# The first loads of an attention and channel-mix kernel on other queues: projection and one k on ScalarE's, the other three on SyncE's

## The chip, the cores and the metric

The kernel runs on one core of a Trainium2 chip. A core has five engines that run side by side, each with its own instruction stream: TensorE (PE in the profile, with PEld for its weight loads), VectorE (DVE), ScalarE (ACT), GpSimd (POOL) and SyncE (SP), which here only issues transfers. Transfers (DMA) are issued by an engine into its own queue and carried out by 16 DMA engines. The metric is the time in microseconds (us) that the device takes for the whole kernel; lower is better.

## The reference

Two parts in a row. First an attention whose mask comes from hashing: each row of q and k (4 batches, 8 heads, 768 rows, 64 wide) is multiplied by a projection of 64 x 6, the signs of the six results make a bucket, and a query sees only the keys of its own bucket.

```python
q_bits = (np.einsum('bhsd,dk->bhsk', q, proj) > 0).astype(np.int64)
k_bits = (np.einsum('bhsd,dk->bhsk', k, proj) > 0).astype(np.int64)
...
mask = q_bucket[:, :, :, None] == k_bucket[:, :, None, :]
scores = scale * np.matmul(q, k.transpose(0, 1, 3, 2))
scores = np.where(mask, scores, -1000000000.0)
...
return np.matmul(attn, v).astype(np.float32)
```

Then a channel mix over the heads put side by side (512 wide): each row is blended with the row before it in two ways, one blend goes through a 512 x 1024 product, a squared ReLU and a 1024 x 512 product, the other through a 512 x 512 product and a sigmoid, and the two results are multiplied.

## The kernel before, in words

The 32 heads are worked in 16 pairs. For each pair, q and k are brought into a transposed form (64 rows per head, 768 columns), and six rows of signs are put beside them, so that one product gives score and mask bonus together. A pair has 12 slots, one for each head and each block of 128 keys: a score product (`score`, L491), an exponential on ScalarE (`pt`, L498), and two slots later the product with the values (`pv`, L528). The channel mix of the batch before is worked in between from a list of items. The order of all work on every engine is written out by hand (`tc.manual_schedule`).

The change lies in the start, ahead of the first slot. These are its steps in program order; pair 0 is handled differently from all others, since nothing can hide its loads.

- The projection `projp` is loaded by a DMA that GpSimd issues (L69), ahead of GpSimd's own work: building two identity matrices, four memsets (L221), and a copy of the projection into the other half of the partitions (L230), which waits for that load.
- `load_qk(0)` (L256) loads q and k of pair 0 in four transfers, a head at a time: q of either head on SyncE's queue, k of either head on ScalarE's.
- ScalarE then loads its table of functions and runs one dummy exponential (L971).
- SyncE goes on with v of the first head (L296), q and k of pair 1 (L262), the two mixing vectors (L975), v of the second head, v of pair 1, and q and k of pair 2.
- TensorE multiplies constants (`keep_warm`, L987), nine products of 128 x 384 whose result is not used.
- `turn_pe` (L331) transposes: q of the first head, then k of the first head, three products each, and ScalarE copies each result to `t` (L335). `cast_pe` turns halves of `t` into the score operands `aq` and `ak` on VectorE, GpSimd or ScalarE (L349, L347).
- `turn_pe` for k of the second head; then `bits_first` (L363), eight products of `t` with the projection for the first head's hash bits; then the signs of these: two on ScalarE for q (L374), two on VectorE for k (L403).
- `turn_pe` for q of the second head, and `turn_and_cast` for q of the first head of pair 1.
- Then slot 0 begins with the first score product (L491).

Each engine works strictly in this order; an instruction that waits holds up all behind it on the same engine. SyncE and ScalarE each have one queue of transfers. A transfer signals its end on one of eight semaphores that all transfers of these two queues use in turn, in program order, and a transfer from SyncE that takes a semaphore for the next time waits until its last user has landed.

Of the kernel before, what the change touches and what calls it, by code (L numbers as in the profile page):

```python
# [36 lines left out]
def kernel(  # L37
# [13 lines left out]
    nc = tc.nc  # L51
    B, H, S, D = q.shape
    NB = proj.shape[1]
    DM = H * D
    DF = moe_w_k.shape[1]
    NC_ = S // P
    HALF = S // 2
# [6 lines left out]
    consts = ctx.enter_context(tc.tile_pool(name="consts", bufs=1))  # L64

    projp = consts.tile([P, 64], FP32, name="projp")
    nc.gpsimd.dma_start(out=projp[0:D, 0:NB], in_=proj)  # L69
    ident32 = consts.tile([P, P], FP32, name="ident32")  # L70
    make_identity(nc, ident32)
    ident16 = consts.tile([P, P], BF16, name="ident16")
# [99 lines left out]
    def fast():  # L172
        with ExitStack() as fx:
# [42 lines left out]
            for s in range(NSET):  # L216
                d = {}
# [29 lines left out]
            SRC = (q, k)  # L247

            def load_qk(n):
                b, t = divmod(n, NPB)  # L250
                tl = nat.tile([P, 2, 2, HALF], FP32, name=f"qk{n}", tag="qk")
                nats[n] = tl
                if n == 0:
                    for j in range(2):
                        for i, eng in enumerate((nc.sync, nc.scalar)):
                            eng.dma_start(  # L256
                                out=tl[:, i, j, :],
                                in_=SRC[i][b, 2 * t + j].rearrange("(p c) d -> p (c d)", c=NC_),
                            )
                    return  # L260
                for i in range(2):
                    nc.sync.dma_start(  # L262
                        out=tl[:, i, :, :],
                        in_=SRC[i][b, 2 * t : 2 * t + 2].rearrange(
                            "j (p c) d -> p j (c d)", c=NC_
                        ),
                    )
# [18 lines left out]
            def load_pair(n, sides="qk"):  # L286
                if n < NTE:
                    load_qk(n)
                else:
                    load_blocks(n, sides)  # L290
# [35 lines left out]
            def turn_pe(n, i, j, eng=None):  # L326

                which, tp = take([P, HALF], FP32, f"tp{n}_{i}_{j}")
                for x in range(3):
                    cols = slice(x * P, (x + 1) * P)  # L330
                    nc.tensor.transpose(tp[:, cols], nats[n][:, i, j, cols], ident32)  # L331
                if eng in (None, nc.vector):
                    nc.vector.tensor_copy(t32(n)[:, i, j, :], tp)
                else:
                    eng.copy(t32(n)[:, i, j, :], tp)  # L335
                give(which)
# [629 lines left out]


            load_qk(0)
            warm = rcp.tile([P, 1], FP32, name="warm", tag="warm")
            nc.vector.memset(warm, 0.0)  # L970
            nc.scalar.activation(warm, warm, AF.Exp)  # L971
            load_v(0, (0,))
            load_qk(1)
            for x, src in enumerate((moe_mu_k, moe_mu_r)):
                nc.sync.dma_start(  # L975
                    out=mu_rows[x * NDC : (x + 1) * NDC, :],
                    in_=src.rearrange("(c p) -> c p", p=P),
# [5 lines left out]
            idle = scp.tile([P, 2, 512], FP32, name="idle", tag="sc")  # L983

            def keep_warm(count, to):
                for _ in range(count):
                    nc.tensor.matmul(  # L987
                        to,
                        epsm,
                        epsm[:, None, :].to_broadcast([P, 3, P]),  # L990
                        start=True,
                        stop=True,
                    )
# [2 lines left out]
                take([P, HALF], FP32, f"bf0{side}") for side in "qk"  # L996
            ]
            firsts[0] = bq, bk
            keep_warm(9, idle[:, 0, 0:HALF])
            turn_pe(0, 0, 0, nc.scalar)  # L1000
            turn_pe(0, 1, 0, nc.scalar)
            cast_pe(0, 0, 0, (nc.vector, nc.gpsimd))
# [259 lines left out]
    with tc.manual_schedule():  # L1262
        fast()
# [33 lines left out]
```

## Time and profile before

| | us |
|---|---|
| median of three runs | 248.12 |
| the three runs | 250.88, 247.43, 248.12 |
| the profiled execution | 249.21 |
| span of that execution, first to last instruction | 247.1 |
| TensorE busy in it | 239.0 (97%) |
| ScalarE busy | 207.7 (84%) |
| VectorE busy | 175.6 (71%) |
| GpSimd busy | 115.6 (47%) |

All times inside the kernel are counted from the start of the span. The profile has a page (busy time by engine, the span in 40 slices, DMA queues, the chain of work that ended last, the costliest groups), and the trace behind it answers finer questions: a timeline of instructions in a window, busy time by window, the chain in order of time, who waited for whom. In a line of the timeline stand start, duration, engine, source line, operation, output and inputs, shapes, a count where equal neighbours are merged, and in brackets how long the engine stood idle before it and what ended that. SPq, ACTq and POOL lines with DMA_DIRECT2D are the issuing of a transfer, not the transfer.

### The profile page before, as it was taken

How to read it: one execution, taken by the hardware profiler on the slowest of the kernel's cores; microseconds unless marked ns; L12 is line 12 of the kernel's file. 1: busy time of each engine (PE TensorE's matmuls, PEld its weight loads, DVE VectorE, ACT ScalarE, POOL GpSimd, SP SyncE). 2: the span in 40 equal slices, each digit the busy share in tenths (PEclk: the TensorE clock that was granted, in tenths of full speed). 3: DMA queues.
4: the chain of work that ended last, by engine and by line, in shares of the span. 5: the costliest groups of instructions: out<-in, count | busy, mean ns of one | idle time of the engine just before them, and what ended most of it. 6: DMA issues, size and time to landing. Idle time of an engine off the chain costs nothing.

```text
span 247.1 us, 6715 instructions
## 1 busy us (share of the span) xinstructions
PE 239.0 (97%) x2443; PEld 144.6 (59%) x2443; DVE 175.6 (71%) x416; ACT 207.7 (84%) x343; POOL 115.6 (47%) x216
## 2 busy tenths in 40 slices
PE   5998999999999999999999999999999999999995
PEld 3565766664665556565665656565665656555443
DVE  2776988969896957577594957686697837499522
ACT  4797999999899888889999889889999898629620
POOL 5898885796919082744519182653709100000000
PEclk9999999999999999999999999999999999999999
DMA  6998897496999385776928386775920111120133
GB/s 191 348 219 196 181 209 189 88 208 139 229 158 263 76 239 137 220 170 169 217 61 220 67 220 144 233 157 156 228 73 5 46 46 42 45 86 1 45 109 112
DMA packets 28230, 36.70 MB, mean 149 GB/s; under 512 B 3216, under 2 KB 25376, under 8 KB 28192
## 3 DMA queue, kind: packets, MB, share of 16 engines
q1 hardware_dynamic: 25744, 33.21, 51.8%
q0 software_dynamic: 2160, 2.62, 6.9%
q8 instruction: 20, 0.33, 0.7%
q10 hardware_dynamic: 288, 0.39, 0.5%
q14 instruction: 18, 0.15, 0.2%
HBM read 31.99 MB, written 6.29 MB: 155 GB/s over the span
## 4 chain that ended last, share of the span: by engine, by line
PE 85%; ACT 8%; DMA 4%; issue 1%; SPq 1%; DVE 0%; ACTq 0%
PE sc L491 22%; PE vp L620 17%; PE kp L620 16%; PE oo L528 12%; PE rp L620 8%; ACT pt L498 7%; PE bb L450 4%; DMA qk<-in_q_dram 3%; PE ot L575 2%; DMA aq<-sg 1%; PE tp L331 1%; PE bb L423 1%; PE oo L519 1%; ACT sq L314 0%; SPq L256 0%
## 5 line engine op out<-in xcount | busy, mean ns | idle before, releaser
L498 ACT ACTIVATE pt<-sc 128x768 bf16<-128x768 f32 x192 | 151.0, 815 | 16.1 <-PE sc L491 13.6
L491 PE MATMUL sc<-aq,ak 70*128 70x384 bf16 (+1 forms) x384 | 93.8, 325 | 1.5 <-ACT pt L498 1.1
L528 PEld LDWEIGHTS <-pt 128*128 128x128 bf16 x1152 | 60.6, 97 | 27.0 <-ACT pt L498 0.2
L528 PE MATMUL oo<-va,pt 128*128 128x65 bf16 x1152 | 66.3, 193 | 0.0
L620 PE MATMUL vp<-wv_sb,k 128*128 128x512 bf16 (+2 forms) x200 | 54.7, 370 | 0.0
L620 PE MATMUL kp<-xk,wk_sb 128*128 128x384 bf16 x256 | 53.6, 326 | 0.4 <-DVE ob L548 0.4
L491 PEld LDWEIGHTS <-ak 70*128 70x128 bf16 (+1 forms) x384 | 34.4, 98 | 27.5 <-issue 4.5
L393 POOL TENSOR_SCALAR aq<-t 64x768 bf16<-64x768 f32 x24 | 19.8, 826 | 56.4 <-DVE t L388 47.2
L657 DVE TENSOR_TENSOR k<-kr 128x384 bf16<-128x384 bf16 x64 | 27.0, 433 | 11.3 <-ACT kr L651 10.7
L620 PEld LDWEIGHTS <-wk_sb 128*128 128x128 bf16 x256 | 21.7, 97 | 14.0 <-issue 3.8
L651 ACT ACTIVATE kr<-kp 128x384 bf16<-128x384 f32 x49 | 24.4, 500 | 4.5 <-PE kp L620 4.5
L620 PE MATMUL rp<-wr_sb,xr 128*128 128x512 bf16 x96 | 27.9, 379 | 0.0
L679 DVE SCALAR_TENSOR_TENSOR os<-th,vp 128x512 f32<-128x512 bf16 (+2 forms) x25 | 16.5, 660 | 15.3 <-PE vp L620 11.9
L620 PEld LDWEIGHTS <-k 128*128 128x128 bf16 x200 | 16.8, 98 | 10.6 <-issue 1.2
L393 POOL TENSOR_SCALAR ak<-t 64x768 bf16<-64x768 f32 x24 | 20.5, 853 | 4.5 <-DVE t L388 1.7
L668 ACT ACTIVATE th<-rp 128x512 bf16<-128x512 f32 x24 | 14.3, 595 | 9.8 <-PE rp L620 9.8
L388 DVE STREAM_TRANSPOSE t<-bl 128x768 f32<-128x768 f32 x24 | 22.4, 957 | 0.0
L477 POOL CAST va<-vf 128x384 bf16<-128x384 f32 x32 | 18.3, 573 | 5.3 <-DMA vf<-in_v_dram 4.5
L314 ACT ACTIVATE sq<-bl 128x768 bf16<-128x768 f32 x24 | 20.2, 844 | 0.0
L479 POOL TENSOR_TENSOR s<-vf 128x192 f32<-128x192 f32 x32 | 20.1, 627 | 0.0
L576 DVE COPY xt<-ot 128x768 bf16<-128x768 bf16 x16 | 8.9, 557 | 14.7 <-PE ot L575 14.7
L541 DVE TENSOR_TENSOR su<-oo,vb 128x390 f32<-128x390 f32 x12 | 6.7, 562 | 10.0 <-PE oo L528 10.0
(87 smaller groups left out, 236.8 us busy)
## 6 DMA issues: line engine op xcount, KB each, us to landing
bl<-in_q_dram SPq DMA_DIRECT2D x48, 176.0 KB
bl<-in_k_dram SPq DMA_DIRECT2D x48, 176.0 KB
vf<-in_v_dram SPq DMA_DIRECT2D x15, 384.0 KB
out_dram<-os SPq DMA_DIRECT2D x18, 256.0 KB
out_dram<-os SPq DMA_DIRECT2D x10, 128.0 KB
qk<-in_q_dram SPq DMA_DIRECT2D x3, 384.0 KB
qk<-in_k_dram SPq DMA_DIRECT2D x3, 384.0 KB
wk_sb<-in_moe_w_k_dram POOLq DMA_DIRECT2D x2, 512.0 KB, 6.4
```

Source lines behind the costliest of these rows:

```text
L314: nc.scalar.activation(junk, src, AF.Square, accum_out=acc)
L388: nc.vector.transpose(t32(n)[:, i].rearrange("p h (c f x) -> p (h c) f x", c=3, f=4), src)
L393: eng.tensor_scalar(out=augs[n % NSET]["qk"[i], j][ROWS[j], :], in0=t32(n)[ROWS[j], i].rearrange("p h y -> p (h y)"), scalar1=(1.0, ALPHA)[i],
L477: nc.gpsimd.tensor_copy(to, of)
L479: nc.gpsimd.tensor_add(s3, vf[:, 0 : 3 * D], vf[:, 3 * D : 6 * D])
L491: nc.tensor.matmul(sc[:, sp, 0:HALF], au["k", j][kr, jc * P : (jc + 1) * P], au["q", j][kr, sp * HALF : (sp + 1) * HALF], start=True, stop ...
L498: nc.scalar.activation(pt.rearrange("p (s q) -> p s q", s=2), sc[:, :, 0:HALF], AF.Exp, bias=EXP_BIAS, scale=SCALE / 2.0 if (n, j) == TWIC ...
L528: nc.tensor.matmul(oo[:, ic, :], pts[n, j, jc][:, ic * P : (ic + 1) * P], vas[n % NSET][j][:, jc, :],  start=(late(n) and jc == 0 and ic = ...
L620: nc.tensor.matmul(box["t"], lhs(), rhs(), start=(i == 0), stop=(i == len(mms) - 1))
L651: nc.scalar.activation(kr, kp, AF.Relu)
L657: 1, lambda: nc.vector.tensor_tensor(out=k2, in0=kr, in1=kr, op=ALU.mult)
L679: nc.vector.scalar_tensor_tensor(out=box["os"][:, y], in0=box["th"][:, y], scalar=1.0, in1=vp, op0=ALU.add, op1=ALU.mult,)
```

## The change

Three edits, all at the start. The projection is loaded from ScalarE's queue rather than by GpSimd. Of the four loads of pair 0, ScalarE's queue keeps one, k of the second head, behind the projection; SyncE's takes q of the first head, k of the first head and q of the second, in this order. TensorE multiplies seven constants rather than nine.

```diff
-    nc.gpsimd.dma_start(out=projp[0:D, 0:NB], in_=proj)
+    nc.scalar.dma_start(out=projp[0:D, 0:NB], in_=proj)
...
                 if n == 0:
-                    for j in range(2):
-                        for i, eng in enumerate((nc.sync, nc.scalar)):
-                            eng.dma_start(
-                                out=tl[:, i, j, :],
-                                in_=SRC[i][b, 2 * t + j].rearrange("(p c) d -> p (c d)", c=NC_),
-                            )
+
+                    for i, j, eng in (
+                        (0, 0, nc.sync), (1, 0, nc.sync), (1, 1, nc.scalar), (0, 1, nc.sync)
+                    ):
+                        eng.dma_start(
+                            out=tl[:, i, j, :],
+                            in_=SRC[i][b, 2 * t + j].rearrange("(p c) d -> p (c d)", c=NC_),
+                        )
                     return
...
-            keep_warm(9, idle[:, 0, 0:HALF])
+            keep_warm(7, idle[:, 0, 0:HALF])
```

In `(i, j)`, `i` is 0 for q and 1 for k, and `j` is the head. The order of instructions on TensorE, VectorE and GpSimd is otherwise the same, and so is ScalarE's behind its two transfers.

## The prediction

> **What bounds the kernel now.** I read the page first. Its engine rows make TensorE (PE) the busiest engine by far, and the chain that ended last names it for most of the span; only 4% of that chain is DMA.
>
> ```profile
> PE 239.0 (97%) x2443; PEld 144.6 (59%) x2443; DVE 175.6 (71%) x416; ACT 207.7 (84%) x343; POOL 115.6 (47%) x216
> ...
> PE 85%; ACT 8%; DMA 4%; issue 1%; SPq 1%; DVE 0%; ACTq 0%
> ```
>
> The reader is to see that no steady part of the kernel is touched by this change: all of it lies ahead of the first score product. So the next views are the windows of the start and the same chain there, listed in order of time.
>
> ```profile
> 0.00:8.82 8.82, 5.77 (x32) 3.04 (x33) 2.79 (x22) 4.61 (x9) 5.62 (x20) 1.00 0.76 241
> 8.82:20.00 11.18, 10.79 (x133) 7.20 (x130) 9.48 (x21) 9.93 (x16) 9.81 (x22) 1.00 0.84 233
> ```
>
> ```profile
> 2.14 6.19 DMA qk<-in_q_dram
> 8.33 0.14 issue
> 8.47 0.52 PE tp L331 x3
> 8.98 0.33 PE sc L491 x2
> 9.31 0.78 PE bf L363 x8
> ```
>
> The columns of the windows are length, then busy time and count of PE, PEld, DVE, ACT and POOL, then clock, DMA share and GB/s. From 8.82 us on, PE is busy 10.79 of 11.18 us; before that, 5.77 of 8.82. What the start is worth is therefore decided by when the first score product begins, at 8.82 us. And the chain says what decided that: not a transfer of pair 0, whose order the change rewrites, but the q of **pair 1**, issued at 2.14 and landed at 8.33. PE works in program order, and three transposes of pair 1 stand ahead of the first score.
>
> The timeline shows the other chain that leads to the same score, through pair 0:
>
> ```profile
> 0.74 0.88 SPq L256 DMA_DIRECT2D qk<-in_q_dram  x2
> 0.74 0.90 ACTq L256 DMA_DIRECT2D qk<-in_k_dram  x2
> 1.05 2.99 PE L987 MATMUL idle<-epsm 128*128 128x384 bf16 x9 [1.05 <-DVE epsm L75]
> 1.27 0.74 POOL L69 DMA_DIRECT2D projp<-in_proj_dram  x1 [0.83 <-POOLq L1281]
> ...
> 3.88 0.82 PE L331 MATMUL tp<-ident,qk 128*128 128x128 f32 x6
> 3.96 0.42 POOL L221 MEMSET ak<- 64x384 f32 x1
> ...
> 4.41 0.86 ACT L335 COPY t<-tp 128x384 f32<-128x384 f32 x2 [1.24 <-PE tp L331]
> ...
> 5.30 0.52 ACT L347 ACTIVATE ak<-t 64x384 bf16<-64x384 f32 x1
> ...
> 6.13 0.52 PE L331 MATMUL tp<-ident,qk 128*128 128x128 f32 x3 [1.44 <-DMA qk<-in_k_dram]
> 6.23 0.18 POOL L230 COPY projp<-projp 64x6 f32<-64x6 f32 x1 [1.85 <-DMA projp<-in_proj_dram]
> ...
> 6.58 0.51 PE L363 MATMUL bf0q<-t,projp 64*32 64x384 f32 x1
> ...
> 7.36 0.55 PE L331 MATMUL tp<-ident,qk 128*128 128x128 f32 x3
> ...
> 7.54 0.98 ACT L374 ACTIVATE aq<-bf0q 6x384 bf16<-6x384 f32 x2 [0.36 <-PE bf0k L363]
> ...
> 8.47 0.52 PE L331 MATMUL tp<-ident,qk 128*128 128x128 f32 x3 [0.56 <-DMA qk<-in_q_dram]
> 8.75 0.75 DVE L349 TENSOR_SCALAR aq<-t 64x384 bf16<-64x384 f32 x2
> 8.82 0.49 PE L491 MATMUL sc<-aq,ak 70*128 70x384 bf16 x2
> ```
>
> PE stands still for 1.44 us until k of the second head has landed (6.13), GpSimd 1.85 us until the projection has (6.23); then come the bit products (6.58) and the signs on ScalarE, which end at 7.54 + 0.98 = 8.52. The change shortens this chain, but the other one ends later: had the signs been there early, the score would still have followed the transposes that started at 8.47. The two are only 8.82 - 8.52 = 0.3 us apart, so neither alone can give more than the other lets it.
>
> **The change, part by part.** The *projection* moves from GpSimd's queue to ScalarE's. GpSimd loses 0.74 us of issuing, so its memsets, done at 3.96 + 0.42 = 4.38, end near 3.6; the identity that the transposes need comes early too, at nothing gained, because they wait for q. On ScalarE's queue it takes a slot of 0.90 / 2 = 0.45 us, exactly that of the k which leaves, so k of the second head keeps its place there and the table load behind it does not move. Its landing by this queue is not in the trace. Bounds: the first q and k, some 130 times its bytes, were transposed 3.88 - 0.74 = 3.1 us after their issue; the old way took 4.8 us.
>
> ```profile
> projp<-in_proj_dram POOLq DMA_DIRECT2D x1, 1.5 KB, 4.8
> ```
>
> I take 3.1 (a hardware queue, at the head of it): landed by 3.9, two microseconds before anything can use it. Its copy on GpSimd no longer binds at all.
>
> *k of the first head* goes second on SyncE's queue: issued 0.88 / 2 = 0.44 us later. Before, its transposes were the last three of six, from 3.88 + 0.33 = 4.2 on. Bounds for them now: 0.44 later (4.65), or no later, since half the bytes no longer share the engines ahead of it. I take the late end, as the second head's k now runs beside it on the other queue: the second copy to t ends at 4.41 + 0.86 + 0.44 = 5.7 instead of 5.27. If nothing covered it, it would cost 0.44 us; it is covered by the transfer that ends at 8.33.
>
> *k of the second head* has only the 1.5 KB of the projection ahead of it on its queue instead of a whole head's k. Bounds for its transposes: 6.13 as now, or right behind the first head's, 4.65 + 0.33 = 5.0. I take the early end. The bit products need both copies, so they start near 5.75 instead of 6.58, and the signs, 7.54 - 6.58 = 0.96 behind, would run from 6.7 to 7.7, not 8.52. *q of the second head* is third on SyncE's queue, 0.44 us later; its transposes (7.36) come behind the bit products and can be late by as much without holding the score past 7.7.
>
> *The rest of SyncE's queue*: v, pair 1's q and k and the two mixing vectors are issued 0.44 us later. The q of pair 1 needs 6.19 us from issue to landing with three transfers ahead of it, so it waits in the queue, not for its issue: cost nothing, as long as the engines have other work. A later SyncE transfer waits for the one eight places before it; with one more hardware transfer these pairs shift by one, so v of the second head waits for k of the second head, not for the first q. GpSimd converts that v at 12.30 us:
>
> ```profile
> 12.30 0.51 POOL L477 CAST va<-vf 128x384 bf16<-128x384 f32 x1
> ```
>
> which leaves over 5 us of cover.
>
> So the sum hangs on **when pair 1's q lands**. Ahead of it go the same bytes as before: four transfers of pair 0 and one of v. What the engines moved meanwhile:
>
> ```profile
> 2.00:4.00 2.00, 2.00 (x9) 0.99 (x8) 0.29 (x14) 1.15 (x2) 1.98 (x9) 1.00 0.99 320
> 4.00:6.00 2.00, 0.70 (x7) 0.46 (x5) 0.35 (x1) 1.38 (x3) 0.38 (x2) 1.00 0.86 228
> 6.00:8.00 2.00, 1.78 (x14) 0.77 (x14) 0.42 (x1) 0.94 (x2) 1.54 (x6) 1.00 1.00 357
> ```
>
> Between 4 and 6 us the rate fell to 228 GB/s and the DMA share to 0.86, with work queued. At the 320 of the window before, the 2 us would have carried 184 KB more, which is 184 / 357 = 0.5 us of the rate behind it. In that window the projection's software-built transfer ran beside the others (it landed just before 6.23), so the change removes one suspect; the trace does not show that it was the cause. Bounds for the landing: unchanged, 8.33, or 1.0 us earlier (the dip gone and the engines level). I take 0.5 us earlier, the size of the dip. Then the transposes start near 8.0 and the score near 8.3, still behind the signs of 7.7. Gain 0.5 us; behind 8.82 PE is full, so it goes through to the end.
>
> A rule of the Trainium skill speaks against even that: "DMA: Bandwidth & Descriptors", section "Issuing engines are not separate DMA queues", says that transfers from all engines run on the same 16 DMA engines, so that spreading them saves issue time only. By it the sum would be 0 us. The trace agrees in that 6.19 us of landing stand against 0.44 us of issue.
>
> *Two of nine constant products* go: the nine start 0.32 us apart (from 1.1 to 3.6 us, eight steps), so PE is free at 1.05 + 7 x 0.32 = 3.3 us rather than 3.9. Nothing waits there but the first transposes, gated by q's landing. Alone they are worth 0 to 0.6 us on pair 0's chain, all covered by the transfer of pair 1; I take 0. What they may cost is the second rival.
>
> ```profile
> L987 PE MATMUL idle<-epsm x9: 454/527/528, 1.1 to 3.6; 128*128 128x384 bf16 x9
> ```
>
> Sum: -0.5 us against the profiled execution, 249.21 us (span 247.1 and 2.1 around it), or 248.7. That execution lies 1.1 us above the median of the three runs, 248.12, so the prediction for a median is 248.12 - 0.5 = **247.6 us**.
>
> **The rivals.** *Nothing moves* (the change does not do what it says): pair 1's q lands at 8.33 whatever goes before it, since the bytes are the same, and the dip is chance. For it: the chain's 6.19 us; against it: the dip itself. Time 248.1.
>
> *Slower, by the clock of PE.* The nine products take 0.32 us for 384 columns, while two score products of 384 columns take 0.33 together: PE began at half speed. The transposes at 3.88 ran as fast as those of 10.73, six in 0.82 us, so the clock had risen by then, after 2.8 us of unbroken products. (The window rows give a clock of 1.00 from the first microsecond on, so that column does not show this.)
>
> ```profile
> 10.57 0.33 PE sc L491 x2
> ```
>
> ```profile
> 10.73 0.82 PE L331 MATMUL tp<-ident,qk 128*128 128x128 f32 x6
> ```
>
> Seven products are 7 x 0.32 = 2.2 us. If the clock needs more than that, it stays low through the gaps of the start and rises only in the dense work behind the first score: some 2.8 to 3.4 us of it at half speed loses 1.4 to 1.7 us, and the bit products ahead, 0.8 us longer, up to 0.3 more. It decides from the point where the products stop before the clock has risen and the transfers leave PE idle. Against it: transposes follow at 3.3 to 4.2 and fill up the sum. Time 248.12 + 1.4 to 2.0, say 249.8. For a loss of 2% (5 us) the clock would have to be low for 10 us of dense work.
>
> On the same point the Trainium skill, "TensorE: Matmul & The Clock Gate", Part 1 (the HAM clock gate), states that the clock is released after about 3.4 us of sustained activity, in a free-running window, and its Part 4 that transposes do not count as activity in the same way; by it the release could slip to a later window in some executions. The 2.8 us above agree with a free-running window, and no run here shows yet what seven products do.
>
> *More gain*: the engines run level, pair 1's q lands by 7.3, and the signs at 7.7 decide: 8.82 - 7.7 = 1.1 us, 247.0. Against it: nothing shows that the transfers of pair 0 were what made some engines late.
>
> **How the numbers follow.** My forecast gets 0.45, nothing moves 0.25, the clock 0.20, more gain 0.10. The likeliest alone spans 246.9 to 248.3 (gain between 0 and 1.0, with 0.2 either way for a median). The runs shown reach from 247.43 to 250.88, a scatter wider than the gain; so the range goes from 246.3 (more gain, with the lowest run's 0.7 below the median) to 250.2 (the clock, at its dear end). Over 2% is 5 us, about what a measurement of this kernel can tell from no change. No case reaches it with its own price. Slower gets 0.10: half of the clock's chance, for executions in which it stays low through several gaps. Faster gets 0.04, for what I have not seen; within 2%: 0.86.
>
> **What would show it.** Right: the chain of waits still names the q of pair 1 ahead of the first score, which starts at 8.0 to 8.6 us; GpSimd's copy of the projection starts before 5 us; the transposes of the second head's k start before 5.6; the window 4 to 6 us moves over 270 GB/s. Wrong: a first score at 8.8 with an unchanged landing (nothing moves); transposes or score products of 0.33 us each, not a pair, behind 3.9 us (the clock); a first score before 7.8, with a sign on ScalarE named just ahead of it (more gain).

## The result, and the profile after

| | before | after |
|---|---|---|
| median of 20 runs, us | 248.09 | 249.25 |
| lowest and highest, us | 247.43, 252.85 | 248.04, 250.66 |
| the profiled execution, us | 249.21 | 249.21 |
| its span, us | 247.1 | 247.3 |
| first score product at | 8.82 | 9.57 |
| first score product of pair 1 at | 20.40 | 20.62 |

The change made the kernel slower by 0.4%: the ratio of after to before is 1.0042, with a 95% interval of 1.0024 to 1.0061. The forecast was 0.2% faster. The two profiled executions took the same time, 249.21 us; the one of before lies 1.1 us above its median, the one of after lies at it. So the profiles show where the time is decided, and the medians how much it is.

First the page of after: the engine row, and the chain that ended last by engine.

```profile
PE 239.4 (97%) x2419; PEld 145.6 (59%) x2441; DVE 175.4 (71%) x416; ACT 207.8 (84%) x343; POOL 114.9 (46%) x215
...
PE 90%; ACT 5%; DVE 2%; issue 1%; ACTq 0%
```

The 4% of DMA are gone from the chain. Then the windows of after, up to its first score product and behind it (columns as in the prediction), and the start of its chain in order of time.

```profile
0.00:9.57 9.57, 7.43 (x30) 3.99 (x31) 2.55 (x21) 4.57 (x9) 5.70 (x21) 1.00 0.79 249
9.57:20.00 10.43, 10.39 (x124) 6.81 (x123) 8.93 (x20) 9.16 (x15) 8.12 (x18) 1.00 0.80 223
```

```profile
1.05 2.42 PE idle L988 x7
3.47 1.45 PE tp L332 x6
6.00 0.88 PE tp L332 x3
...
8.31 1.47 PE tp L332 x6
```

TensorE does less work ahead of the first score than before (30 instructions, not 32) and is busy longer, 7.43 us against 5.77. This chain names no transfer, only TensorE's own slow instructions and two of ScalarE's; its link at 6.00 hides a transfer, as the rows below show. The timeline of after shows two faults, a late k and a slow TensorE:

```profile
0.74 0.55 ACTq L68 DMA_DIRECT2D projp<-in_proj_dram  x1
1.33 0.60 ACTq L257 DMA_DIRECT2D qk<-in_k_dram  x1
...
3.40 1.51 PE L332 MATMUL tp<-ident,qk 128*128 128x128 f32 x6
3.59 0.18 POOL L229 COPY projp<-projp 64x6 f32<-64x6 f32 x1 [0.51 <-DMA projp<-in_proj_dram]
...
5.88 0.84 SPq L297 DMA_DIRECT2D vf<-in_v_dram  x2
6.00 0.88 PE L332 MATMUL tp<-ident,qk 128*128 128x128 f32 x3 [1.09 <-ACT ak L348]
6.81 0.85 PE L364 MATMUL bf0q<-t,projp 64*32 64x384 f32 x1
...
8.24 1.54 PE L332 MATMUL tp<-ident,qk 128*128 128x128 f32 x6
9.57 0.79 PE L492 MATMUL sc<-aq,ak 70*128 70x384 bf16 x2
```

The projection is there early, as forecast: GpSimd copies it at 3.59, not 6.23. But k of the second head, whose way was meant to be free, is transposed at 6.00, against 6.13 before and 5.0 in the forecast, and SyncE stands until then as well (5.88; before, it issued v of the second head at 4.17). And everything on TensorE runs at half speed up to the first score: six transposes in 1.51 us instead of 0.82, a product of the bits in 0.85 instead of 0.51. (The bracket of the row at 6.00 names ScalarE. But by the trace's records the k landed at 5.87, SyncE's v at 5.88 waits for the same k, and in a second execution of this kernel, below, the bracket names the transfer.)

The 6.13 of before is itself a late one. By the same records the second head's k landed at 6.00 in that profile, but at 4.78 to 5.47 in the five other profiles below that keep before's queues (with seven, twelve or three products, the gap filled, the later block loads). In the six with after's queues it landed at 5.71 to 6.28. One profile of each kernel therefore hides most of what the change did to this load.

Behind the start nothing differs. This is the first score product of pair 1, in after:

```profile
20.62 0.49 PE L492 MATMUL sc<-aq,ak 70*128 70x384 bf16 x2
```

From it to the end of the span are 247.3 - 20.6 = 226.7 us, and as much in before, 247.1 - 20.4. In 17 of the 20 profiles of this study that rest is 226.6 to 226.9 us (the three others are named below). So **the kernel's time is decided by when pair 1's first score product starts**, and that has two conditions: the work from the first score on, 10.8 us of it when nothing waits and the clock is up (20.49 - 9.66 in a second execution of after), and the sign rows of pair 1, which SyncE loads. In before the second ended last:

```profile
20.40 0.48 PE L491 MATMUL sc<-aq,ak 70*128 70x384 bf16 x2 [0.75 <-ACT pt L498]
```

The 0.75 us of idle time are a wait for these rows (issued at 14.64 and 15.53 behind a row of long transfers). By the trace's records they landed at 20.31, and the product starts 0.09 us behind them, exactly as in a run further down whose bracket names them (landed 19.09, started 19.18). The exponential that the bracket names here ended at 20.38, but the product does not need it: in that other run it starts before the same exponential has ended. Without that wait the first score at 8.82 would have meant 19.65.

### The profile page after: what moved, and what is told of

The parts are those of the page before. It is cut to its first block, busy times and chain, and to the rows that moved or that the text cites. A ratio compares the mean times of both kernels' runs of the same rounds, so it can differ in the third digit from the quotient of the medians.

```text
span 247.3 us, 6689 instructions
## 1 busy us (share of the span) xinstructions
PE 239.4 (97%) x2419; PEld 145.6 (59%) x2441; DVE 175.4 (71%) x416; ACT 207.8 (84%) x343; POOL 114.9 (46%) x215
## 4 chain that ended last, share of the span: by engine, by line
PE 90%; ACT 5%; DVE 2%; issue 1%; ACTq 0%
PE sc L492 24%; PE kp L621 16%; PE vp L621 16%; PE oo L529 12%; PE rp L621 8%; ACT pt L499 5%; PE bb L451 4%; PE tp L332 3%; PE ot L576 2%; PE oo L520 1%; PE idle L988 1%; PE bb L424 1%; PE bf0q L364 1%; DVE xr L609 0%; PE bf L364 0%
## 5 line engine op out<-in xcount | busy, mean ns | idle before, releaser
L621 PE MATMUL vp<-wv_sb,k 128*128 128x512 bf16 (+2 forms) x184 | 50.7, 370 | 0.7 <-issue 0.2
L621 PE MATMUL rp<-wr_sb,xr 128*128 128x512 bf16 x90 | 26.9, 379 | 0.3
```

The costliest lines, as they stand in the source:

```text
L621: nc.tensor.matmul(box["t"], lhs(), rhs(), start=(i == 0), stop=(i == len(mms) - 1))
```

## The experiments

Three causes could make the start slower: the projection at the head of ScalarE's queue, the new order of the four loads, and the two products fewer. The rivals in all that follows are the clock (products too few, or gaps) and the transfers (something lands later). Ratios are to the kernel before, measured beside it.

### The number of constant products

Four kernels: the new queues with nine and with twelve products, the old queues with seven and with twelve.

```diff
-            keep_warm(7, idle[:, 0, 0:HALF])
+            keep_warm(9, idle[:, 0, 0:HALF])
```

> The changed queues with the nine constant products of before. Clock theory (the loss is the late rise of TensorE's clock, brought by two products fewer): the rise comes back to about 4 us, the transposes behind it take 0.11 us each, the first score starts at 8.2 to 8.9 us, ratio to before 0.997 to 1.001. Queue theory (the loss is in the new order of the transfers, the clock only happened to be late in the profiled execution): the ratio stays at 1.003 to 1.006.

> The queues of before with seven products. Clock theory: the clock rises only behind 7 us, single score products of 0.33 us at the start, first score at 9.3 to 9.8 us, ratio 1.003 to 1.006. Queue theory: nothing waits for these products, since q lands at 3.7 us; ratio 0.999 to 1.001.

> The changed queues with twelve products, which last until 1.05 + 12 x 0.32 = 4.9 us. Clock theory: the clock has surely risen by 4.9, the transposes of q wait for the products by 1.6 us but the first score waits for pair 1's q at 8.2 and starts at 8.3 to 8.9, ratio 0.996 to 1.001. Queue theory: 1.003 to 1.008, the products adding their own delay.

> The queues of before with twelve products. Clock theory: the clock rises early in every execution, the second head's k at 6.1 still gates the signs, first score at 8.8, ratio 0.997 to 1.000 and fewer slow executions than before. Queue theory: 1.000 to 1.003, since the products only delay the first transposes by 1 us.

Measured: new queues with nine 1.0019 (0.9993 to 1.0046) and with twelve 1.0026 (1.0000 to 1.0052); old queues with seven 1.0013 (0.9988 to 1.0038) and with twelve 1.0014 (0.9991 to 1.0036). In all four profiles the bits ran at full speed, also with seven on the old queues. This is one line of the new queues with nine, the second head's k:

```profile
6.42 0.52 PE L332 MATMUL tp<-ident,qk 128*128 128x128 f32 x3 [1.55 <-DMA qk<-in_k_dram]
```

With the clock up, the k still comes late, at 6.42, so the lateness is not the clock's doing. And a clock that is up does not bring pair 1 forward here. In the two profiles with the new queues the first score starts at 8.56 and 8.35, earlier than in before, but pair 1 at 20.68 and 20.41, as late as in after (nine products, then twelve):

```profile
20.68 0.48 PE L492 MATMUL sc<-aq,ak 70*128 70x384 bf16 x2 [1.17 <-POOL aq L350]
20.41 0.48 PE L492 MATMUL sc<-aq,ak 70*128 70x384 bf16 x2 [0.81 <-ACT pt L499]
```

TensorE stands idle for 1.17 and 0.81 us. By the trace's records pair 1's signs landed at 20.59 and 20.32, again 0.09 us ahead of the product: it is the second gate, whatever the brackets name. In after the signs landed at 20.02 and the product started at 20.62, so there the late first score decided. Each ratio alone holds no change or nearly; on the old queues neither seven nor twelve moved the time measurably. Two further kernels went further on this line: before with three products only, and after with four more products in TensorE's gap behind the first six transposes.

```diff
             turn_pe(0, 1, 0, nc.scalar)
+            keep_warm(4, idle[:, 1, 0:HALF])
```

> The queues of before with three constant products, so that TensorE stands idle from 2.0 to 3.7 us. Clock theory: the clock rises only in the dense work behind the first score, first score at 9.3 to 9.8 us, ratio 1.003 to 1.008. Gate theory: 0.999 to 1.001, since nothing waits for these products.

> The changed kernel with four more constant products in the gap behind the transposes of the first head, where TensorE waits for k of the second head. Clock theory: busy almost without a gap from 1.05 to 6, so the clock rises by 7 us at the latest, ratio 0.998 to 1.001. Gate theory: no effect, 1.003 to 1.006.

Three products: 1.0024 (1.0013 to 1.0035), with bits at 0.85 us each and the first score still at 8.75, since the transfers came early in that execution. After with its gap filled: 1.0030 (1.0016 to 1.0044). In its profile the clock is mended, and the k is as late as in after:

```profile
6.08 0.52 PE L332 MATMUL tp<-ident,qk 128*128 128x128 f32 x3
6.53 0.51 PE L364 MATMUL bf0q<-t,projp 64*32 64x384 f32 x1
...
8.84 0.49 PE L492 MATMUL sc<-aq,ak 70*128 70x384 bf16 x2
```

The clock explains the step of the first score from 8.8 to 9.6 in the profile, but mending it gave back at most a part of the 0.4%.

### Lighter traffic ahead of pair 1's signs

Before and after, each with the first loads for pair 4, which stand ahead of pair 1's signs on SyncE's queue, moved five slots later.

```diff
                     lambda: load_pair(3, "qk"),
-                    lambda: load_pair(4, "q"),
...
                     lambda: load_v(2),
+                    lambda: load_pair(4, "q"),
```

> The kernel before, with the four q block loads of pair 4 issued behind the sign copies of pair 1, not ahead of them: a second gate (the first score of pair 1 waits until 20.3 us for signs that queue behind those loads) is taken away. Both theories: the signs land near 17.7 us, the wait of 0.75 us at 20.4 goes, ratio 0.996 to 0.999.

> The changed kernel with the same later block loads. Start theory (the loss is in the late first score of pair 0, by the clock and the transfers ahead of it; the second gate only hides part of it): it stays 0.6 to 1.4 us slower than the kernel before with the same edit, ratio 0.999 to 1.003. Gate theory (the loss is that the signs of pair 1 land later behind a fuller SyncE queue): no slower than the kernel before with the same edit, within 0.3 us, ratio 0.996 to 0.999.

Before with it: 1.0057 (1.0031 to 1.0083); after with it: 1.0077 (1.0054 to 1.0099). The wait at pair 1 goes (its first product at 19.16 in before's variant), but pair 2 then waits for its own signs, 1.06 and 1.22 us, and starts at 30.55 and 31.93, against 30.41 and 30.63 in before and after: the rest behind pair 1's first product is 247.1 - 19.2 = 227.9 us in both, 1.2 longer than in the 17. These are two of the three exceptions to the constant rest. The gate is a real one, but this is no way around it.

### Projection and order apart

Three kernels with nine products. The first moves only the projection's load to ScalarE's queue, at its head. The second makes only the change of the four loads and leaves the projection on GpSimd. The third has the new order with the projection on ScalarE's queue, but *behind* the k of the second head:

```diff
-    nc.gpsimd.dma_start(out=projp[0:D, 0:NB], in_=proj)
...
             load_qk(0)
+            nc.scalar.dma_start(out=projp[0:D, 0:NB], in_=proj)
+            nc.gpsimd.tensor_copy(projp[D:P, NB : 2 * NB], projp[0:D, 0:NB])
```

In it GpSimd's copy (L230) moves down along with the load, and SyncE's order is the same, q, k, q.

> The kernel before with one edit: the projection is loaded on ScalarE's queue, ahead of its k of the first head, and no longer on GpSimd's; nine products. Supply theory (the projection's 64 short rows at the head of ScalarE's queue hold up the k behind it, and with it SyncE's v of the second head and all transfers behind that): the first k lands 0.4 to 0.9 us later than in before, the k of the second head lands at 5.5 to 6.2, 2.9 to 3.2 MB have moved by 12 us, ratio 1.002 to 1.006. Order theory (the move of the first head's k to SyncE's queue costs the time, not the projection): ratio 0.999 to 1.001, with 3.2 MB or more by 12 us.

> The kernel before with the other edit: q and k of the first head and q of the second on SyncE's queue, k of the second head on ScalarE's, as in the kernel after; the projection stays on GpSimd's queue; nine products. Supply theory: nothing stands ahead of the k of the second head, it lands by 4.2, 3.3 MB or more by 12 us, ratio 0.997 to 1.000. Order theory: the k of the first head lands later than in before, the first scores come later than 8.82, ratio 1.001 to 1.004.

> The order of the kernel after, with k of the second head issued first on ScalarE's queue, the projection behind it on the same queue, and GpSimd's copy of the projection moved behind that load; nine products. Supply theory: as the run with the order alone, the k of the second head lands by 4.2, SyncE's v of the second head is issued by 4.5, ratio 0.996 to 1.000. Order theory: ratio 1.001 to 1.004, as with the order alone.

Measured: projection alone 251.17 us, 1.0120 (1.0085 to 1.0154); order alone 248.12 us, 0.9999 (0.9981 to 1.0017); projection behind 247.76 us, 0.9976 (0.9956 to 0.9996). (In the profiled execution of the order alone the granted clock is 0.50 from 22.8 to 29.5 us, so only its start is used; it is the third exception.) The order theory falls, and the projection alone costs more than I had expected of it and almost three times what the whole change cost. Its timeline, of an execution that took 249.68 us, the fastest of the six:

```profile
6.05 0.90 PE L331 MATMUL tp<-ident,qk 128*128 128x128 f32 x3 [1.29 <-DMA qk<-in_k_dram]
7.20 0.88 PE L331 MATMUL tp<-ident,qk 128*128 128x128 f32 x3 [0.25 <-DMA qk<-in_k_dram]
8.00 0.85 PE L363 MATMUL bf0q<-t,projp 64*32 64x384 f32 x1
...
10.35 0.62 PE L491 MATMUL sc<-aq,ak 70*128 70x384 bf16 x2
```

Here both k stand behind the projection on ScalarE's queue, and both are late: the first, which before was transposed together with q at about 4.2, now at 6.05, the second at 7.20. In the order of after, only one k stands behind it; the other rides on SyncE's queue, and was there for the six transposes from 3.40 on. So the new order, harmless in itself, gives back most of what the projection costs (1.0019 with nine products). In the kernel with the projection behind, the k is transposed at 5.57, and what holds it is a copy on ScalarE, not a transfer:

```profile
5.57 0.55 PE L330 MATMUL tp<-ident,qk 128*128 128x128 f32 x3 [0.20 <-ACT t L334]
```

The fourth kernel is before with its own gap filled in the same way:

> The kernel before with four more products of constants behind the transposes of k of the first head, where TensorE waits. Clock theory (idle time of TensorE in the first 8 us costs speed behind it): the clock stays up through the gap, the first scores come at 8.6 to 8.9, ratio 0.997 to 1.000. If the gap's idle time does not matter to the clock in before: first scores at 8.8 to 9.2 (the four products take their own time), ratio 1.000 to 1.002.

It measured 1.0003 (0.9985 to 1.0021), first score at 9.34: in before, whose clock is up, filling the gap gained nothing.

### Rows or place, and what is the clock's

Four kernels on one chip: the projection behind, with seven products; the projection alone at the head, with the four products in the gap; the order alone, with the same 1.5 KB as *two rows* at the head of ScalarE's queue, into a tile that nothing reads; and after itself.

```diff
+    row = consts.tile([2, D * NB // 2], FP32, name="row")
+    nc.scalar.dma_start(out=row, in_=proj.rearrange("(o a) b -> o (a b)", o=2))
```

> The order in which the projection stands behind the k of the second head on ScalarE's queue, with seven products of constants. If seven products are harmful only where a late k leaves TensorE idle behind them: no such gap here, the clock has risen by 7 us (four products of the bits at 0.51 us or less each), ratio 0.996 to 1.000. If seven are too few in themselves: the bits take 0.84 us each as in the kernel after, the first scores come after 9.2, ratio 1.001 to 1.004.

> The kernel before with the projection at the head of ScalarE's queue (the run that took 1.2% more), and four products of constants in the gap behind the transposes of the first k. Splits that loss. Clock theory: the products of the bits take 0.51 us instead of 0.85, the first scores come 0.8 to 1.5 us earlier than 10.36, ratio 1.004 to 1.009. Supply theory alone: clock up, but ratio stays 1.010 to 1.014, since the transfers are as late as without the fillers.

> The run with the order alone, with one more small load at the head of ScalarE's queue: the same 1.5 KB of the projection as two rows of 768 bytes, into a tile that nothing reads (the projection that is used still comes on GpSimd's queue). Theory of the rows (64 rows of 24 bytes are what holds up the k behind them): the k of the second head lands by 4.4 and the ratio is 0.998 to 1.001. Theory of the place (any transfer ahead does it, by its 0.4 to 0.6 us of issue): the k of the second head lands at 5.5 or later, ratio 1.001 to 1.004.

> The kernel after, unchanged, on the same chip as the three others of this call, so that their ratios can be set beside its own: 1.002 to 1.006, first scores at 9.2 to 9.8, k of the second head landed at 5.6 to 6.3, products of the bits at 0.84 us each.

After came to 1.0034 (1.0008 to 1.0060) here, and its second profile names what the first did not:

```profile
6.18 0.88 PE L332 MATMUL tp<-ident,qk 128*128 128x128 f32 x3 [1.42 <-DMA qk<-in_k_dram]
```

*Two rows ahead*: 0.9987 (0.9972 to 1.0001), and all nine transposes of pair 0 run in one go, the k's own, the last three, at 5.33:

```profile
3.91 2.05 PE L334 MATMUL tp<-ident,qk 128*128 128x128 f32 x9
5.89 0.51 PE L366 MATMUL bf0q<-t,projp 64*32 64x384 f32 x1
...
7.65 0.58 PE L494 MATMUL sc<-aq,ak 70*128 70x384 bf16 x2
...
19.18 0.48 PE L494 MATMUL sc<-aq,ak 70*128 70x384 bf16 x2 [0.31 <-DMA ak<-sg]
```

The same bytes at the same place, with 0.53 us of issue against 0.55, do no harm. It is the 64 short rows of 24 bytes that hold up what follows on their queue, not the place. (Two rows may also go through fewer of the 16 DMA engines than 64 do; the trace does not name the engines, so this is not separated from the number of rows.) (The last row shows the second gate by its name: pair 1 waits for its signs.)

*Seven, projection behind*: 1.0017 (0.9995 to 1.0039), against 0.9976 with nine. I had put the harm of seven products down to the late k; here there is none, and yet:

```profile
1.05 2.42 PE L988 MATMUL idle<-epsm 128*128 128x384 bf16 x7 [1.05 <-DVE projp L74]
4.16 2.34 PE L330 MATMUL tp<-ident,qk 128*128 128x128 f32 x9 [0.68 <-DMA qk<-in_q_dram]
6.43 0.85 PE L362 MATMUL bf0q<-t,projp 64*32 64x384 f32 x1
```

Seven products end at 3.47, q is there only at 4.16, and the clock stays down through the bits. With nine, the products reach to 4.1 and the bits run at 0.51. In this pair of executions the two products bridged that gap. Reaching the first operand is not enough in itself: in after the seven reach it as well (3.40), and with the projection alone the nine do (3.90), but behind the transposes TensorE then waits for a k, and both run the bits at 0.85.

*Projection at the head, gap filled*: 1.0077 (1.0053 to 1.0101) instead of 1.0120, first score at 9.51 instead of 10.35, bits at 0.51. By the medians a third of that loss was the clock and two thirds are the late transfers themselves; the two intervals overlap a little, so the split is rough.

### By which path the late k costs

A transfer from SyncE that takes over the semaphore of the late k waits for it, and what SyncE issues behind it comes later. The first kernel takes this hold away from the projection-at-the-head kernel: the two mixing vectors' loads move behind q and k of pair 2, so both v take other semaphores. The second does the same to the kernel with the projection behind.

```diff
             load_qk(1)
+            load_v(0, (1,))
+            load_v(1)
+            load_qk(2)
             for x, src in enumerate((moe_mu_k, moe_mu_r)):
...
-            load_v(0, (1,))
-            load_v(1)
-            load_qk(2)
```

> The kernel before with the projection at the head of ScalarE's queue (the run that took 1.2% more), and the loads of the two mixing vectors moved behind q and k of pair 2 on SyncE's queue. So v of the second head and v of pair 1 take the semaphores of the projection and of the first q, and SyncE issues both by 4.6 instead of from 6.02 on; the first transfer that waits for the late k is q of pair 2. Theory of the hold (the late k costs by holding SyncE's issuing): about 0.5 MB more is issued before the hold, the rate between 9 and 11 us no longer falls below 200 GB/s, ratio 1.004 to 1.009. Theory of the landing alone (the late k delays the transposes and the clock, what SyncE issues behind is queued anyway): ratio 1.010 to 1.014.

> The order in which the projection stands behind the k of the second head (0.9976 with nine products), with the same move of the two mixing vectors. Both theories: no late k there, so nothing or a little: ratio 0.994 to 0.999. If the mixing vectors' move delays them so that the work that uses them waits, or the two v ahead of q and k of pair 2 cost more than they did: above 1.000.

The hold went: SyncE issued both v from 3.26 instead of 6.02, and the rate from 8 to 10 us rose from 267 to 372 GB/s. The time hardly did: 1.0100 (1.0055 to 1.0146) beside 1.0120. A small part for the hold is not excluded by that interval, but my theory that it is the main path falls for this kernel: here the late landing costs through TensorE, whose first score comes so late that pair 1's signs are there before they are needed (landed 20.29, used at 22.41). Where the clock is up and the first score early, as with nine and twelve products on the new queues, the signs were the gate; the hold was not taken away there, so what it costs them is not shown. Its windows show that more plainly than any other run (the third column from the right is the granted clock):

```profile
6.00:8.00 2.00, 0.55 (x3) 0.31 (x3) 0.00 (x0) 0.65 (x2) 0.12 (x1) 0.96 1.04 386
8.00:10.00 2.00, 1.91 (x11) 0.70 (x11) 0.00 (x0) 0.83 (x2) 1.84 (x5) 0.50 1.04 372
10.00:12.00 2.00, 2.00 (x16) 1.34 (x16) 1.25 (x3) 1.45 (x4) 0.18 (x1) 0.69 1.05 366
```

With both k late, TensorE works 0.55 us out of two between 6 and 8 us, and the clock, which was up, falls to 0.50 just when the work arrives. The first score comes at 11.47, and the span is 249.0.

The second kernel measured 247.59 us, 0.9977 (0.9960 to 0.9995): as fast as the one with the projection behind and no faster. These two are the only versions whose interval lies below 1, by 0.2% against before, and each ends just short of it.

## Why the prediction was wrong

**The step that failed** is k of the second head: "has only the 1.5 KB of the projection ahead of it on its queue instead of a whole head's k", for which I took transposes at 5.0. I counted the projection by its bytes and its slot of issue. It is 64 rows of 24 bytes, and the k behind them on the same queue landed at 5.71 to 6.28 and was transposed at 5.85 to 6.42 (after and its variants with that order); with the same bytes in two rows it landed at 4.49 and was transposed at 5.33. I had bounded this step by 6.13 and 5.0 and took the early end with no row that showed short rows ahead of a long transfer. The bound for "as now" was bad luck: in five other executions with before's queues this k landed 0.5 to 1.2 us earlier than in the one that I read, so there was less to gain than it showed. The slot of issue was not equal either: 0.55 us, not 0.45, with 0.60 for the k behind it, so the table load started at 1.96, not 1.67.

**The gain itself**, 0.5 us from an earlier landing of pair 1's q, failed too: by the trace's records of transfers it landed at 8.22 for 8.33. Between 4 and 6 us the engines moved 267 GB/s, just short of the 270 that I had asked for.

**The two products** were taken at nothing, with the clock as a rival at 0.20. That rival is what the profile of after shows, smaller than I priced it (1.7 us): the first score came 0.75 us later. Its condition was put rightly, that the products stop before the clock has risen and the transfers leave TensorE idle. The four corners, each measured beside before but not all on one chip, with the projection ahead or behind in the new order: nine products 1.0019 and 0.9976, seven 1.0042 and 1.0017. Either way round, the rows cost 0.25 to 0.4% and the two products 0.2 to 0.4%. Each single difference is about as wide as its uncertainty; that both corners of the change together cost 0.66% is clear. Before itself lies between the corners; in its order the second k stands behind the first.

**What was right**: the projection landed early and its copy stopped binding (3.59; forecast before 5). The first head's k was not in the way. The second transfer of v did wait for k of the second head, as forecast, and taking such a wait away gave nothing that could be measured. SyncE's 0.44 us of later issue did not show either. The transposes of pair 1's q followed the second head's at once (8.24, six in a row), so it no longer bound. The order alone, loads spread otherwise, moved nothing: 0.9999. That agrees with the rule weighed there, the Trainium skill's "Issuing engines are not separate DMA queues" ("DMA: Bandwidth & Descriptors"). The projection alone does not: moved to another queue it cost 1.2%, and there the measurement decides.

**What the sum left out**: "behind 8.82 PE is full, so it goes through to the end". There was a second gate at 20.40, where TensorE stood for 0.75 us in the very profile that I read, beyond the windows that I quoted. An earlier first score is worth something only up to the landing of pair 1's signs. With two rows ahead the first score came 1.17 us earlier than in before, at 7.65, and the median ratio was 0.9987. (In the range, 250.2 is 0.1 above its own sum, 248.12 + 2.0.)

**What stays open**: first, what in the queue makes the tail. By the trace's records of transfers, the 64 rows are moved by 2.9 us and take 9 ns each; half of the k's rows behind them have started by 3.7 us, but the last only at 5.4, while with the projection behind the last starts at 3.7. The rows' own time does not explain that, and the trace does not say which of the 16 engines came last. Second, what sets the landing of pair 1's signs. They landed at 20.31 to 20.59 us in three profiles whose second k was late, but at 19.73 in a fourth (after with its gap filled), and at 20.83 with the order alone, whose k landed at 3.74.

## What to carry to other kernels

Count a small load by its rows and by what follows it on its queue, not by its bytes: put a transfer of many short rows behind the ones that the first work waits for, or load it in few rows. Before taking away products that only keep TensorE busy, look at what time the first real operand lands in several executions, and at the gap behind it: in the runs here neither a total nor reaching that point was enough by itself. Read a start in more than one execution before pricing it: the one read here had its k later than the five others of the same queues. And when a gain is carried through to the end, look for the next wait further down the timeline, past the stage that the change touches.

## What the runs showed of the hardware

- The clock can come late or be lost again within one start. It rose early or late with the same seven products (bits at 0.51 us with the old queues, 0.85 in after). Six runs of the kernel with the projection alone reach from 249.68 to 252.30 us, with mean granted clocks from 1.000 down to 0.986 in the longest; the clock is not all of that spread, since a run at 1.000 took 251.40.
- In the traces the granted clock changes only at the ends of steps of about 3.41 us, whose place differs between executions. These are two of the steps in the first kernel without the hold (columns as in the prediction):

```profile
4.42:7.83 3.41, 0.78 (x5) 0.31 (x3) 0.35 (x1) 0.96 (x3) 0.67 (x1) 1.00 0.98 347
7.83:11.25 3.42, 3.16 (x16) 1.62 (x17) 0.55 (x1) 1.72 (x4) 2.14 (x5) 0.50 1.05 371
```

- Behind 0.78 us of work the clock is halved for the next step, behind 3.16 us it is full again. Counted back in such steps from the rise that each trace records, the step up to 3.84 in before held 2.79 us of work and raised the clock. The two up to 3.34 and 6.76 in after held 2.29 and 2.33 and did not, nor did the one up to 6.87 with seven products and the projection behind, with 2.74. With seven on the old queues a step happened to run from 1.04 to 4.45; it held 3.14 us and raised it. So how many products suffice depended on where the steps lay. This is an inference from these few traces.
- On this the Trainium skill, "TensorE: Matmul & The Clock Gate", Part 1, says that the clock is judged in a free-running window of about 3.4 us, so that the same kernel starts differently from run to run, and that it falls after an idle window. The trace agrees on the window and the spread; but in that kernel without the hold it fell although TensorE's longest idle time was 2.08 us, with 0.55 us of transposes behind it. Whether transposes count as activity there is not settled by these runs.
- Transfers of one kernel land at different times from one execution to the next: pair 1's q was transposed from 8.94 on in a run of before's queues with twelve products, and from 7.94 on in the one with seven.
